# Loading queries and keys in token halves, transposing with a PSUM column step, and a shorter path for the gate's running sums

## The chip, the cores and the metric

The kernel runs on one core of a Trainium2 chip, as one program. The core has a matrix engine (TensorE, PE in the profile; its weight loads are the row PEld), three engines for elementwise work (VectorE or DVE, ScalarE or ACT, GpSimd or POOL), and SyncE (SP), which here issues almost all data transfers. Each engine takes its instructions in the order in which they were written to its queue, and waits on semaphores for the others. PSUM is the memory that PE writes its results to; ACT and DVE read it and write SBUF, from which PE reads again.

The metric is the device time of one execution in microseconds (us), median of three runs.

## The reference

Three layers follow each other. B, H, S, D = 4, 8, 576, 64.

```python
# 1. causal attention with a bias from running sums of a gate s
scores = matmul(q, k.T) / sqrt(D)
cum = cumsum(maximum(s, 0), axis=-1)
bias = -(cum[:, :, :, None] - cum[:, :, None, :])
scores = where(causal, -1e9, scores + minimum(bias, 0))
x = softmax(scores) @ v                      # -> (B, S, H*D)
# 2. gated MLP with a product over tokens
h = gelu(x @ w_in);  u, v = halves of h
v_s = einsum('ts,bsd->btd', w_sg, layernorm(v) * g_ln) + b_sg
x = x + (u * v_s) @ w_out
# 3. one of 8 experts per token; a token may reuse the choice of the token before it
e = argmax(x @ w_gate) or the previous e, by sigmoid(x @ w_local)
out = p[e] * (relu(x @ w1[e]) @ w2[e])
```

Products are computed as sums of products of a high part (type fp32r) and a remainder, so most fp32 tensors are split into `hi` and `lo`: one engine (ACT) writes `hi`, another (DVE) subtracts it from the source and writes `lo`.

## The kernel before

The 32 heads (4 batches x 8) are worked off in 16 pairs; a pair's two heads lie on partitions 0 to 63 and 64 to 127. Attention fills the first part of the program. The gated MLP of a batch (`M_steps`) and its routing (`O_steps`) are woven into the attention of the next batch, and the experts come last, from about 440 us on. The Python generators set the order in which work is emitted; the framework's scheduler then places the instructions on each engine's queue, and `behind(x, name)` tells it to place x after another instruction of the same engine.

**Loading and transposing a pair.** `prep_load(p)` loads a pair's queries and keys into the tiles `nq` and `nk`, one transfer each. Partition `p` of such a tile holds the six tokens 6p to 6p+5, so 96 partitions hold all 576 tokens. `prep_T(p, c)` (c = 0, 1) takes three of the six slots. For each of `nq` and `nk`, PE transposes the three slots into 96 columns each of a PSUM tile (L344), ACT writes the high part into the tile `qk` (L353 for queries, L356 for keys), and DVE writes the remainder (L354, L357). Since slot r of partition p is token 6p+r, the 96 columns of a slot go to every sixth token of the destination:

```python
            def v6(x):
                return x.rearrange("p (t r) -> p r t", r=6)[:, 3 * c:3 * c + 3, :]
```

So each move reads 288 columns of PSUM in a row and writes 288 elements with a step of six (24 bytes). There are 16 pairs x 2 halves x 2 tiles = 64 moves on ACT, as many on DVE, and 192 transposes on PE.

**Scores, softmax and product.** Scores of the first four pairs (batch 0) are made by `emit_R` (L466), those of the others by `emit_S` and `emit_tail` (L841, a helper's line, which is used by all later layers too). DVE takes each row's extreme (L411), ACT the exponential (L417), POOL and DVE the reciprocal of the sum (L418, L419), POOL the scaling (L420). PE transposes the result (L502); in batch 0 DVE or ACT copies it to the tile `et` (L508, L506); then PE multiplies with the values (L541).

**The gate's running sums.** Batch 0 needs its sums early: `emit_first` loads eight rows of the gate (tile `u`, L200), and makes the sums and their split (L223 to L233) with a scan along the row (L224). All other heads get theirs from `emit_cum`, at the pair p = 2: it loads all 32 heads' rows into 32 partitions, clamps (L239), scans (L241), and then for each of five query blocks subtracts the sum at the block's start, 32 partitions at a time (L246). The two results of 128 and 32 rows are split (L247 on ACT, L248 on DVE) and stored to `cum_d` in DRAM, from where the assembly of the later heads (`prep_asm`, `prep_cum`) reads.

**Other constants.** `emit_consts2` makes small constants for the routing (L309 to L330): POOL writes integers into a scratch tile, DVE converts them. They are needed only from the first `O_steps` on. W_steps also splits the 64-bit weights `w_in` (`vg`, L723 to L730) and prepares `bbc` (L1400) while batch 0's attention runs.

Of the kernel before, what the change touches and what calls it, by code (L numbers as in the profile page):

```python
# [33 lines left out]
def kernel(  # L34
# [217 lines left out]
    cum_rows = cum_d.rearrange("z (i g) s -> g (z i) s", g=NH)  # L252
    GD = H
    SW = ()

    def cblk(g):

        return 64 * (g % 2) + 16 * (g // 2)
# [1259 lines left out]
```

## Time and profile before

| | |
|---|---|
| median of 3 runs | 843.71 us (842.79 to 845.37) |
| profiled execution, its own time | 844.22 us |
| its span, first to last instruction | 842.4 us |
| mean granted TensorE clock | 0.978 of full speed |
| PE busy | 792.2 us (94%) |
| DVE, ACT, POOL busy | 532.1 (63%), 449.9 (53%), 349.1 us (41%) |

The profile is of one execution: its time less its span, 1.8 us, lies outside the first and last instruction. Busy time of an engine is the union of its instructions, and a share of the span is an average over stages that differ; a PE that is busy is not always at its peak.

### The profile page before, as it was taken

To read this page: it belongs to the slowest core of one execution; us is meant where nothing else is said; L and a number is where in the kernel's file an instruction comes from. 1 tells how busy PE (TensorE), PEld (TensorE's weight loads), DVE (VectorE), ACT (ScalarE), POOL (GpSimd) and SP (SyncE) were. 2 spreads that over 40 slices of the span, in tenths; PEclk is the share of its full clock that TensorE was granted. 3 is DMA by queue.
4 is the path that set the end of the run, shared out by engine and by line. 5 is a ranking of instruction groups with operands and counts; after the bars stand their busy time and mean duration, and the time that the engine had idled before them with its cause. 6 is when DMAs were issued, how large, how long until landed. Compare 5 with 4: busy or idle time off the path is not lost. (4 is left out here: it accounts for less than half of the span.)

```text
span 842.4 us, 14677 instructions
## 1 busy us (share of the span) xinstructions
PE 792.2 (94%) x4828; PEld 678.2 (80%) x4828; DVE 532.1 (63%) x1489; ACT 449.9 (53%) x1040; POOL 349.1 (41%) x627
## 2 busy tenths in 40 slices
PE   8797998989999999999998999989999999999995
PEld 4564687779879889878788788778989989899894
DVE  7777577876768788867786476774555444353420
ACT  5676577766637786527784245134454344443510
POOL 5785556576434387614586001052022222313101
PEclk9699999999999999999999999999999999999998
DMA  8565699794488587587450763144564544535300
GB/s 186 137 184 142 153 229 306 192 237 99 93 192 231 153 214 174 130 238 201 92 179 18 255 220 123 51 139 142 178 211 122 176 127 146 186 126 184 125 5 35
DMA packets 117735, 133.33 MB, mean 158 GB/s; under 512 B 69184, under 2 KB 82624, under 8 KB 117656
## 3 DMA queue, kind: packets, MB, share of 16 engines
q1 hardware_dynamic: 113816, 122.87, 53.6%
q0 software_dynamic: 3840, 9.48, 3.0%
q8 instruction: 40, 0.66, 0.3%
q14 instruction: 39, 0.32, 0.1%
HBM read 91.07 MB, written 23.13 MB: 136 GB/s over the span
## 5 line engine op out<-in xcount | busy, mean ns | idle before, releaser
L1211 DVE TENSOR_TENSOR wp<-wraw,wp 128x1024 fp32r<-128x1024 f32 x63 | 76.6, 1223 | 96.6 <-ACT wp L1210 96.0
L841 PE MATMUL ps<-wp,hT 128*128 128x512 f32 x528 | 123.0, 392 | 0.0
L1267 POOL DMA_INDIRECT out_dram<-y,ids x24 | 34.9, 1454 | 204.6 <-ACT y L1266 157.0
L841 PE MATMUL ps<-xT,wp 128*128 128x384 f32 x672 | 119.1, 336 | 0.0
L841 PEld LDWEIGHTS ps<-xT,wp 128*128 128x128 f32 x672 | 117.3, 188 | 0.7
L841 PEld LDWEIGHTS ps<-wp,hT 128*128 128x128 f32 x528 | 98.6, 188 | 21.1
L1210 ACT CAST wp<-wraw 128x1024 fp32r<-128x1024 f32 x64 | 66.5, 1050 | 65.3 <-DMA wraw<-in_moe_w_dram 58.6
L417 ACT ACTIVATE E<-E,negm 128x128 f32<-128x128 f32 (+4 forms) x136 | 79.1, 582 | 35.5 <-DVE negm L411 30.5
L420 POOL TENSOR_SCALAR E<-E,lsum 128x128 f32<-128x128 f32 (+4 forms) x136 | 79.6, 588 | 38.1 <-DVE lsum L419 28.4
L541 PE MATMUL ps<-et,vv 128*128 128x320 f32 (+9 forms) x476 | 82.7, 314 | 9.9 <-DVE et L508 5.7
L418 POOL TENSOR_SCALAR lsum<-lsum 128x1 f32<-128x1 f32 x144 | 34.5, 240 | 124.7 <-ACT E L417 111.2
L541 PEld LDWEIGHTS ps<-et,vv 128*128 128x128 f32 (+1 forms) x476 | 65.1, 171 | 25.1 <-ACT wsg L247 5.4
L502 PE MATMUL ps<-ident,E 128*128 128x128 f32 (+1 forms) x452 | 69.2, 266 | 8.9 <-POOL E L420 5.5
L411 DVE CUSTOM_DVE_ANT_0 E<-ps,zmask 128x128 f32<-128x128 f32 (+4 forms) x136 | 63.5, 474 | 17.8 <-PE ps L841 15.4
L841 PE MATMUL ps<-wsg,vg 128*128 128x288 f32 x448 | 68.3, 304 | 2.0 <-DVE g L850 1.0
L510 ACT CAST et<-ps 128x384 fp32r<-128x384 f32 (+3 forms) x120 | 50.6, 431 | 33.4 <-PE ps L502 31.4
L841 PEld LDWEIGHTS ps<-wsg,vg 128*128 128x128 f32 x448 | 62.3, 192 | 3.3 <-DVE g L850 1.2
L502 PEld LDWEIGHTS ps<-ident,E 128*128 128x128 f32 (+1 forms) x452 | 48.0, 142 | 20.6 <-POOL E L420 6.9
L511 DVE TENSOR_TENSOR et<-ps,et 128x384 fp32r<-128x384 f32 (+3 forms) x120 | 56.8, 483 | 7.2 <-ACT et L510 6.8
L841 PE MATMUL ps<-xh,w 128*128 128x288 f32 x256 | 57.6, 303 | 0.6 <-DVE negm L411 0.5
L1255 DVE SCALAR_TENSOR_TENSOR hT<-ps,hT 128x384 fp32r<-128x384 f32 x56 | 30.3, 553 | 40.4 <-ACT hT L1254 40.4
L841 PE MATMUL ps<-w,vg 128*128 128x512 f32 (+1 forms) x216 | 54.5, 396 | 0.0
(305 smaller groups left out, 1624.7 us busy)
## 6 DMA issues: line engine op xcount, KB each, us to landing
wraw<-in_moe_w_dram SPq DMA_DIRECT2D x64, 512.0 KB
qk<-qk SPq DMA_DIRECT2D x24, 432.0 KB
w<-wv_d SPq DMA_DIRECT2D x16, 512.0 KB
w<-wo_d SPq DMA_DIRECT2D x16, 512.0 KB
qk<-qk SPq DMA_DIRECT2D x24, 288.0 KB
w<-wu_d SPq DMA_DIRECT2D x12, 512.0 KB
nq<-in_q_dram SPq DMA_DIRECT2D x16, 288.0 KB
nk<-in_k_dram SPq DMA_DIRECT2D x16, 288.0 KB
```

The source lines that it names most:

```text
L411: hred[g] = DVE.tensor_tensor_reduce(out=e[:, a:z], in0=pt[:, 0:z - a], in1=zmask[:, m0:m0 + z - a], scale=-1.0, scalar=BIG if hi == 0 els ...
L417: ACT.activation(out=x, in_=x, func=ACTF.Exp, scale=-1.0, bias=nm, accum_out=l)
L418: POOL.tensor_scalar(out=l, in0=l, scalar1=1e-9, scalar2=0.0, op0=ALU.add, op1=ALU.add)
L420: POOL.tensor_scalar(out=x, in0=x, scalar1=l, scalar2=1.0, op0=ALU.mult, op1=ALU.mult)
L502: PE.transpose(pt[:, j * M:(j + 1) * M], e[h, 128 * j:128 * (j + 1)], ident[h, h])
L510: ACT.copy(out=dst[0], in_=src)
L511: DVE.tensor_tensor(out=dst[1], in0=src, in1=f32v(dst[0]), op=ALU.subtract)
L541: PE.matmul(x, lhsT=l, rhs=rhs if g >= F4 else f32v(rhs), start=(j == 0 and n_ == 0), stop=(j == js[-1] and n_ == len(ms) - 1),)
L841: ms = [PE.matmul(pt, lhsT=l, rhs=r, start=(first_ and x == 0), stop=(last_ and x == n - 1)) for x, (l, r) in enumerate(pairs)]
L1210: c = ACT.copy(out=w[:, 0, :], in_=r)
L1211: a = (POOL if (e, j) == (0, KD) else DVE).tensor_tensor(out=w[:, 1, :], in0=r, in1=f32v(w[:, 0, :]), op=ALU.subtract)
L1267: POOL.indirect_dma_start(out=of[:, :], out_offset=bass.IndirectOffsetOnAxis(ap=idx, axis=0), in_=y, in_offset=None, bounds_check=NT - 1, ...
```

## The change

- `prep_load` makes two transfers of each, of 288 tokens: partition p of the first half holds tokens 3p to 3p+2, and of the second half tokens 288+3p to 288+3p+2.
- `prep_T` lets the transpose of slot r write the columns r, r+3, r+6, ... of the PSUM tile (a step of 12 bytes). The PSUM columns then stand in token order, and each move reads 288 elements in a row and writes 288 in a row.
- `emit_cum` leaves out the first eight heads, which never read `cum_d`. It loads the other 24 heads' rows five times, onto 120 partitions, so one clamp, one scan, one subtraction (with a per-partition reference taken by three small operations) and one split take the place of the five subtractions and two splits. `cum_d` has 120 rows in place of 160, and is stored by one transfer.
- the DVE part of `emit_consts2` is placed behind the first pair's first row extremes (`hred[1]`).

```diff
     def emit_cum():
-        R = 128 // NH
-        s_sb = T(mp, [128, S], F32, "u2", bufs=5)[0:NH]
-        dma(s_sb, s.rearrange("b h s -> (b h) s"))
-        behind(DVE.tensor_scalar_max(out=s_sb, in0=s_sb, scalar1=0.0), hred[max(hred)].ins.name)
-        cum = s_sb
-        DVE.tensor_tensor_scan(out=cum, data0=one[0:NH], data1=s_sb, initial=0.0, op0=ALU.mult, op1=ALU.add)
-        for P, i0, z0 in ((128, 0, 6), (NH, R, 8)):
-            tmp = T(mp, [128, S], F32, "u2", bufs=5)
-            ch = wsg[0:P, z0:z0 + 2, :]
-            for a in range(P // NH):
-                DVE.tensor_scalar(out=tmp[NH * a:NH * a + NH], in0=cum, scalar1=cum[:, 128 * (i0 + a):128 * (i0 + a) + 1], scalar2=None, op0=ALU.subtract)
-            ACT.copy(out=ch[:, 0, :], in_=tmp[0:P])
-            DVE.tensor_tensor(out=ch[:, 1, :], in0=tmp[0:P], in1=f32v(ch[:, 0, :]), op=ALU.subtract)
-            dma(cum_d[:, NH * i0:NH * i0 + P, :].rearrange("z p s -> p z s"), ch)
+        n = NH - H
+        P = NQ * n
+        rows, cum = [T(mp, [128, S], F32, "u2", bufs=5)[0:P] for _ in range(2)]
+        src = s.rearrange("b h s -> (b h) s")[H:NH]
+        for i in range(NQ):
+            dma(rows[n * i:n * i + n], src)
+        behind(DVE.tensor_scalar_max(out=rows, in0=rows, scalar1=0.0), hred[max(hred)].ins.name)
+        DVE.tensor_tensor_scan(out=cum, data0=one[0:P], data1=rows, initial=0.0, op0=ALU.mult, op1=ALU.add)
+        m = T(mp, [128, NQ], F32, "m5")[0:P]
+        ref = T(mp, [128, 1], F32, "mr")[0:P]
+        DVE.tensor_reduce(out=m, in_=ident[0:P, 0:P].rearrange("p (i c) -> p i c", c=n), axis=AX.X, op=ALU.add)
+        DVE.tensor_tensor(out=m, in0=cum.rearrange("p (i c) -> p i c", c=64)[:, 0::2, 0], in1=m, op=ALU.mult)
+        DVE.tensor_reduce(out=ref, in_=m, axis=AX.X, op=ALU.add)
+        DVE.tensor_scalar(out=rows, in0=cum, scalar1=ref, scalar2=None, op0=ALU.subtract)
+        ch = wsg[0:P, 6:8, :]
+        ACT.copy(out=ch[:, 0, :], in_=rows)
+        DVE.tensor_tensor(out=ch[:, 1, :], in0=rows, in1=f32v(ch[:, 0, :]), op=ALU.subtract)
+        dma(cum_d.rearrange("z p s -> p z s"), ch)
...
             t = T(ap_, [96, 6, 2, D], F32, nm)
-            dma(t, src[b, h0:h0 + 2].rearrange("h (p r) d -> p r h d", p=96))
+            for a in range(2):
+                dma(t[:, 3 * a:3 * a + 3], src[b, h0:h0 + 2, HS * a:HS * a + HS].rearrange("h (p r) d -> p r h d", p=96))
...
     def emit_consts2():
+        def late_(x):
+            behind(x, hred[1].ins.name)
...
-        DVE.tensor_copy(out=w8d, in_=it[:, 0:8])
+        late_(DVE.tensor_copy(out=w8d, in_=it[:, 0:8]))
...
             for r in range(3):
-                PE.transpose(pt[:, 96 * r:96 * r + 96], n[:, 3 * c + r].rearrange("p h d -> p (h d)"), ident[0:96, 0:96])
-
-            def v6(x):
-                return x.rearrange("p (t r) -> p r t", r=6)[:, 3 * c:3 * c + 3, :]
-
-            src = pt[:, 0:HS].rearrange("p (r t) -> p r t", r=3)
-            hi = v6(t[:, a, :])
-            lo = v6(t[:, 2 + a, :])
+                PE.transpose(
+                    pt[:, 0:HS].rearrange("p (t r) -> p r t", r=3)[:, r], n[:, 3 * c + r].rearrange("p h d -> p (h d)"), ident[0:96, 0:96]
+                )
+            src = pt[:, 0:HS]
+            hi, lo = [t[:, z, HS * c:HS * c + HS] for z in (a, 2 + a)]
```

The line numbers of the changed kernel are one lower in this region (L353 and L356 are its DVE moves, L410 the row extremes, L507 the copies to `et`, L729 the remainder of the weights' split) and by a few more in `emit_cum` and `emit_consts2`.

**Place 1: DVE at `emit_cum`.** Before, from the clamp of the rows (L239) to the copies that feed the next product (L508):

```order
L239 TENSOR_SCALAR u_142_890<-u_142_890 32x576
L508 COPY et_425<-ps 128x3x128
L241 SCALAR_TENSOR_TENSOR u_142_890<-u_38_148,u_142_890 32x576
L730 TENSOR_TENSOR vg_831<-vg_831 128x512
L411 ISA E_148_946,negm_948<-ps,zmask_73 128x512
L246 TENSOR_SCALAR u_143_894<-u_142_890 32x576 x3
L246 TENSOR_SCALAR u_143_894<-u_142_890 32x576
L246 TENSOR_SCALAR u_144_902<-u_142_890 32x576
L411 ISA ga_947,negm_949<-ps,zmask_73 128x512
L508 COPY et_425<-ps 128x5x64
L508 COPY et_425<-ps 128x128
```

The same place in the changed kernel:

```order
L242 TENSOR_SCALAR u_142_898<-u_142_898 120x576
L507 COPY et_431<-ps 128x3x128
L243 SCALAR_TENSOR_TENSOR u_143_899<-u_38_150,u_142_898 120x576
L729 TENSOR_TENSOR vg_839<-vg_839 128x512
L410 ISA E_149_957,negm_959<-ps,zmask_73 128x512
L247 TENSOR_TENSOR m_144_907<-u_143_899,m_144_907 120x5
L410 ISA ga_958,negm_960<-ps,zmask_73 128x512
L507 COPY et_431<-ps 128x5x64
L507 COPY et_431<-ps 128x128
L410 ISA E_28_100,negm_995<-ps,zmask_73 128x288
L248 TENSOR_REDUCE mr_908<-m_144_907 120x1
L249 TENSOR_SCALAR u_142_898<-u_143_899,mr_908 120x576
```

The five subtractions L246 are gone from ahead of the two copies to `et`; one small product stands there, and the single subtraction (L249) comes behind the copies.

**Place 2: SP's queue at the start.** Before (`u` is the gate's rows, `vg` the weights w_in, `vv`, `vt` and `vr` values):

```order
L78 DMA nq_134<-in_q_dram 96x12x64
L78 DMA nk_136<-in_k_dram 96x12x64
L200 DMA u_39_159<-in_s_dram 16x576 x8
L78 DMA vt_105<-in_v_dram 64x4x64
L78 DMA nq_227<-in_q_dram 96x12x64
L78 DMA nk_229<-in_k_dram 96x12x64
L78 DMA vg_363<-in_moe_w_in_dram 128x1024
L78 DMA u_142_890<-in_s_dram 32x576
L78 DMA bbc_75<-in_moe_b_sg_dram 128x576
L78 DMA nq_384<-in_q_dram 96x12x64
L78 DMA nk_386<-in_k_dram 96x12x64
L78 DMA vg_542<-in_moe_w_in_dram 128x1024
```

In the changed kernel (the same stretch; rows that repeat others are left out in both):

```order
L78 DMA nq_134<-in_q_dram 96x6x64 x2
L78 DMA nk_137<-in_k_dram 96x6x64 x2
L200 DMA u_39_161<-in_s_dram 16x576 x8
L78 DMA nq_229<-in_q_dram 96x6x64 x2
L78 DMA nk_232<-in_k_dram 96x6x64 x2
L78 DMA vt_105<-in_v_dram 64x4x64
L78 DMA vg_367<-in_moe_w_in_dram 128x1024
L78 DMA nq_388<-in_q_dram 96x6x64 x2
L78 DMA nk_391<-in_k_dram 96x6x64 x2
L78 DMA u_142_898<-in_s_dram 24x576 x5
L78 DMA bbc_75<-in_moe_b_sg_dram 128x576
L78 DMA vg_548<-in_moe_w_in_dram 128x1024
```

Two more issues stand ahead of the gate's eight rows, twelve more ahead of `bbc`, and ten more ahead of the fourth piece of w_in. Over the whole program SP issues 35 transfers more.

**Place 3: DVE from the first moves to the gate's split.** Before, the sums' clamp (L223) and scan (L224) stand among moves and constants:

```order
L354 SCALAR_TENSOR_TENSOR qk_25_97<-ps,qk_25_97 128x3x96
L309 CAST w8d_78<-ga_268 128x8
L357 TENSOR_TENSOR qk_25_97<-ps,qk_25_97 128x3x96
L312 CAST io_8_79<-ga_268 128x128
L223 TENSOR_SCALAR u_39_159<-u_39_159 128x576
L354 SCALAR_TENSOR_TENSOR qk_25_97<-ps,qk_25_97 128x3x96
L313 CAST ioc_80<-ga_268 128x144
L357 TENSOR_TENSOR qk_25_97<-ps,qk_25_97 128x3x96
L321 TENSOR_SCALAR ltri_86<-io_8_79,pidx_81 128x128
L224 SCALAR_TENSOR_TENSOR u_40_160<-u_38_148,u_39_159 128x576
```

In the changed kernel the moves come first, and the constants after the first row extremes:

```order
L353 SCALAR_TENSOR_TENSOR qk_25_97<-ps,qk_25_97 128x288
L356 TENSOR_TENSOR qk_25_97<-ps,qk_25_97 128x288
L223 TENSOR_SCALAR u_39_161<-u_39_161 128x576
L224 SCALAR_TENSOR_TENSOR u_40_162<-u_38_150,u_39_161 128x576
L233 SCALAR_TENSOR_TENSOR wsg_149<-wsg_149,m_45_175,u_41_163 128x576
L410 ISA E_55_245,negm_247<-ps,zmask_73 128x128
L311 CAST w8d_78<-ga_272 128x8
L314 CAST io_8_79<-ga_272 128x128
L315 CAST ioc_80<-ga_272 128x144
L323 TENSOR_SCALAR ltri_86<-io_8_79,pidx_81 128x128
```

All four moves of the first pair now stand ahead of the clamp, and none of the eleven constants.

## Rows read from the trace of the kernel before

**Rows 1.** Windows: us, then PE, PEld, DVE, ACT, POOL busy, clock, DMA, GB/s.

```profile
0.00:100.00 100.00, 84.40 (x480) 55.20 (x481) 70.98 (x230) 62.23 (x157) 66.82 (x143) 0.90 0.66 159
100.00:440.00 340.00, 322.78 (x2222) 282.20 (x2221) 262.61 (x845) 228.54 (x608) 191.33 (x403) 0.99 0.72 185
440.00:842.40 402.40, 384.98 (x2131) 340.74 (x2129) 198.53 (x415) 159.15 (x275) 91.00 (x84) 0.99 0.42 135
```

**Rows 2.** ACT by shapes: xcount | busy us, mean ns | idle before.

```profile
L356 ACT CAST qk<-ps 128x288 fp32r<-128x288 f32 x32 | 24.3, 758 | 0.9 <-PE ps L344 0.9
L353 ACT ACTIVATE qk<-ps 128x288 fp32r<-128x288 f32 x32 | 22.5, 704 | 7.2 <-PE ps L344 5.9 <-POOL lsum L418 1.0
...
L510 ACT CAST et<-ps 128x320 fp32r<-128x320 f32 x24 | 10.2, 425 | 10.9 <-PE ps L502 9.5 <-PE ps L541 1.1
...
L510 ACT CAST et<-ps 128x256 fp32r<-128x256 f32 x24 | 8.9, 371 | 0.2
```

**Rows 3.** DVE by shapes, the same columns.

```profile
L354 DVE SCALAR_TENSOR_TENSOR qk<-ps,qk 128x288 fp32r<-128x288 f32 x32 | 22.6, 707 | 6.6 <-ACT qk L353 6.3
L357 DVE TENSOR_TENSOR qk<-ps,qk 128x288 fp32r<-128x288 f32 x32 | 22.2, 694 | 0.7 <-ACT qk L356 0.7
...
L511 DVE TENSOR_TENSOR et<-ps,et 128x320 fp32r<-128x320 f32 x24 | 11.6, 483 | 3.7 <-ACT et L510 3.4
...
L511 DVE TENSOR_TENSOR et<-ps,et 128x256 fp32r<-128x256 f32 x24 | 10.0, 418 | 0.3 <-ACT et L510 0.3
```

**Rows 4.** PE's waits, 0 to 100 us: us in total, times, longest.

```profile
PE ps L541 <- DVE et L508: 5.7, 2, 5.2
...
PE ps L466 <- DVE qk L354: 1.4, 2, 1.1
```

**Rows 5.** DVE in order of time at `emit_cum`: start us, us, instruction.

```profile
67.72 1.60 DVE L246 TENSOR_SCALAR u<-u 32x576 f32<-32x576 f32 x3
...
69.54 1.27 DVE L246 TENSOR_SCALAR u<-u 32x576 f32<-32x576 f32 x2
...
71.34 0.67 DVE L508 COPY et<-ps 128x320 f32<-128x320 f32 x2
```

**Rows 6.** PE in order of time, 66 to 84 us; in brackets its idle time before.

```profile
71.96 3.61 PE L541 MATMUL ps<-et,vv 128*64 128x320 f32 x10 [5.19 <-DVE et L508]
...
77.73 0.41 PE L344 MATMUL ps<-ident,nq 96*128 96x96 f32 x3
...
83.53 2.27 PE L541 MATMUL ps<-et,vv 128*64 128x320 f32 x10
```

**Rows 7.** Window of that product; columns as in rows 1.

```profile
71.90:75.50 3.60, 3.54 (x10) 1.80 (x10) 2.44 (x10) 1.23 (x4) 2.82 (x4) 0.61 0.41 157
```

**Rows 8.** SP's issues in order of time, first 26 us.

```profile
2.31 4.43 SPq L200 DMA_DIRECT2D u<-in_s_dram  x8
...
7.63 0.61 SPq L78 DMA_DIRECT2D nq<-in_q_dram  x1
...
16.48 2.62 SPq L78 DMA_DIRECT2D bbc<-in_moe_b_sg_dram  x1
```

**Rows 9.** DVE in order of time, 6 to 27 us.

```profile
6.96 0.16 DVE L309 CAST w8d<-ga 128x8 f32<-128x8 int32 x1
...
8.74 0.45 DVE L223 TENSOR_SCALAR u<-u 128x576 f32<-128x576 f32 x1
...
12.16 0.17 DVE L319 CAST wtok<-ga 128x20 f32<-128x20 int32 x1
...
13.70 0.82 DVE L233 SCALAR_TENSOR_TENSOR wsg<-wsg,m,u 128x576 fp32r<-128x576 f32 x1 [0.18 <-ACT wsg L231]
...
25.45 1.44 DVE L1400 TENSOR_SCALAR bbc<-bbc 128x576 f32<-128x576 f32 x1
```

**Rows 10.** Window of the weights' split beside batch 0; columns as in rows 1.

```profile
17.00:37.40 20.40, 14.87 (x79) 10.77 (x78) 19.55 (x57) 15.01 (x40) 18.37 (x31) 0.67 0.61 142
```

**Rows 11.** Transposes of queries: duration ns min/median/max, first and last start.

```profile
L344 PE MATMUL ps<-ident,nq x96: 243/246/423, 4.9 to 411.0; 96*128 96x96 f32 x96
```

More of the change, by code (lines that the diff above doesn't have):

```diff
@@ L188 @@
     vt = T(ap_, [128, 4, D], F32, "vt")
-    cum_d = dram.tile([2, NQ * NH, S], F32, name="cum_d")
+    cum_d = dram.tile([2, NQ * (NH - H), S], F32, name="cum_d")
     def slot(z, dt=F32R):
@@ L197, in emit_first @@
         rows, cum, t1 = [T(mp, [128, S], F32, "u2", bufs=5) for _ in range(3)]
-        for g in range(GD):
-            z = cblk(g)
-            (POOL if g in SW else SP).dma_start(out=rows[z:z + 16], in_=s[0, g:g + 1, :].to_broadcast([16, S]))
+        for g in range(H):
+            z = 64 * (g % 2) + 16 * (g // 2)
+            SP.dma_start(out=rows[z:z + 16], in_=s[0, g:g + 1, :].to_broadcast([16, S]))
         e = [T(mp, [128, NQ], F32, f"e{z}") for z in range(3)]
@@ L251 @@
-    KX = 64 + 2 * NQ
[L252 to L258, printed above, removed]
+        n = NH - H
[5 more added lines that the diff above has]
+        behind(DVE.tensor_scalar_max(out=rows, in0=rows, scalar1=0.0), hred[max(hred)].ins.name)
@@ L260 @@
+        ch = wsg[0:P, 6:8, :]
+        ACT.copy(out=ch[:, 0, :], in_=rows)
+        DVE.tensor_tensor(out=ch[:, 1, :], in0=rows, in1=f32v(ch[:, 0, :]), op=ALU.subtract)
+        dma(cum_d.rearrange("z p s -> p z s"), ch)
+    KX = 64 + 2 * NQ
+    cum_rows = cum_d.rearrange("z (i g) s -> g (z i) s", g=NH - H)
     last = {(PR - 2 + z) % 2: 2 * PR - 3 + 2 * z for z in range(2)}
@@ L308, in emit_consts2 @@
         POOL.iota(it[:, 320:320 + B * NQ], pattern=[[-S, B], [-128, NQ]], base=FREE, channel_multiplier=-1)
-        DVE.tensor_copy(out=w8d, in_=it[:, 0:8])
-        DVE.tensor_copy(out=s8, in_=it[:, 8:8 + NQ])
-        DVE.tensor_copy(out=pidx, in_=it[:, 16:17])
-        DVE.tensor_copy(out=io128, in_=it[:, 32:160])
-        DVE.tensor_copy(out=ioc, in_=it[:, 160:160 + NC])
+        late_(DVE.tensor_copy(out=w8d, in_=it[:, 0:8]))
+        late_(DVE.tensor_copy(out=s8, in_=it[:, 8:8 + NQ]))
+        late_(DVE.tensor_copy(out=pidx, in_=it[:, 16:17]))
+        late_(DVE.tensor_copy(out=io128, in_=it[:, 32:160]))
+        late_(DVE.tensor_copy(out=ioc, in_=it[:, 160:160 + NC]))
         tk = it[:, 320:320 + B * NQ]
         hl = it[:, 384:384 + B * NQ]
-        DVE.tensor_scalar(out=hl, in0=tk, scalar1=6, scalar2=None, op0=ALU.logical_shift_right)
-        DVE.tensor_copy(out=wtok[:, 0], in_=hl)
-        DVE.tensor_scalar(out=tk, in0=tk, scalar1=63, scalar2=None, op0=ALU.bitwise_and)
-        DVE.tensor_copy(out=wtok[:, 1], in_=tk)
-        DVE.tensor_scalar(out=first, in0=s8, scalar1=9.0, scalar2=None, op0=ALU.is_equal)
-        DVE.tensor_scalar(out=ltri, in0=io128, scalar1=pidx, scalar2=None, op0=ALU.is_gt)
+        late_(DVE.tensor_scalar(out=hl, in0=tk, scalar1=6, scalar2=None, op0=ALU.logical_shift_right))
+        late_(DVE.tensor_copy(out=wtok[:, 0], in_=hl))
+        late_(DVE.tensor_scalar(out=tk, in0=tk, scalar1=63, scalar2=None, op0=ALU.bitwise_and))
+        late_(DVE.tensor_copy(out=wtok[:, 1], in_=tk))
+        late_(DVE.tensor_scalar(out=first, in0=s8, scalar1=9.0, scalar2=None, op0=ALU.is_equal))
+        late_(DVE.tensor_scalar(out=ltri, in0=io128, scalar1=pidx, scalar2=None, op0=ALU.is_gt))
         POOL.memset(onesb, 1.0)
@@ L327, in emit_consts2 @@
         n = E + 1
-        DVE.tensor_tensor(out=ii, in0=ident[0:2 * n, 0:n], in1=ident[0:2 * n, n:2 * n], op=ALU.add)
+        late_(DVE.tensor_tensor(out=ii, in0=ident[0:2 * n, 0:n], in1=ident[0:2 * n, n:2 * n], op=ALU.add))
         dma_after(1, gcol, g_ln.rearrange("(k p) -> p k", p=128))
-        DVE.tensor_scalar(out=gcol, in0=gcol, scalar1=0.5, scalar2=None, op0=ALU.mult)
+        late_(DVE.tensor_scalar(out=gcol, in0=gcol, scalar1=0.5, scalar2=None, op0=ALU.mult))
     Tst = {}
@@ L366, in prep_asm @@
         rs = slice(64 * r, 64 * r + 64)
-        dma(dst[64:KX, 3, :], cum_rows[g])
+        dma(dst[64:KX, 3, :], cum_rows[g - H])
         if buf[g] not in selected:
@@ L377, in prep_cum @@
         for r in range(2):
-            dma(czp[64 * r:64 * r + 2, :], cum_rows[2 * p + r, NQ - 1::NQ, :])
+            dma(czp[64 * r:64 * r + 2, :], cum_rows[2 * p + r - H, NQ - 1::NQ, :])
     VG = 4
```

## The prediction

> **What bounds the kernel now.** I read the windows by stage first: PE is busy for 84.4 + 322.8 + 385.0 = 792.2 us, 94% of the span [rows 1]. A shorter instruction on DVE or ACT therefore gains only where PE is seen to wait for it, and an instruction that gets longer on PE costs nearly its full length. The same windows say where waits are: of the first 100 us PE is idle for 15.6 (100 less 84.4), of the 340 us up to 440 for 17.2, and behind that for 17.4 of 402 in the experts, which the change doesn't touch [rows 1]. DVE is busy for 71% of the first stage and 77% of the second, so these two are where DVE's queue can hold PE up. The chain of waits ends in the experts' last store and says nothing of attention, so I went to PE's waits in the first 100 us: the longest is for copies to `et` by DVE, and a smaller sum is for the transposed queries [rows 4].
>
> **The moves.** 64 moves on each of ACT and DVE write with a step before and in a row after. The trace has no move of 288 columns in a row into fp32r from PSUM; the copies to `et` bracket it, of 256 and 320 columns. On ACT these take 371 and 425 ns, so I take 398 for 288, against 704 and 758: 306 and 360 less, over 32 of each 21.3 us of ACT's time [rows 2]. On DVE 418 and 483 ns give 450 against 707 and 694: 257 and 244 less, 16.0 us [rows 3]. From below, a move might be bound by reading PSUM and not get faster at all; the copies read PSUM too, so I keep this only as a rival.
>
> Most of this lies beside a busy PE. In the first 100 us PE waited for the moves directly 1.4 us in two waits, of 1.1 and 0.3 [rows 4]. Each stands behind one move on ACT and one on DVE in series, about 0.6 together, so the first loses 0.6 and the second all of its 0.3: **0.9 us**. From 100 to 440 us no single wait is the moves' own. Eleven pairs take 11 us off DVE's 262.6 and 14.6 off ACT's 228.5, 4 and 6% of queues that PE waits for. As a share of the 17.2 us of idle that is about 0.9; if one DVE move of each half pair lay on the path it would be 11 x 2 x 0.25 = 5.5; from below it is nothing. I take **1.5**, near the share, since PE's idle there is many short waits.
>
> **The running sums.** PE stood for 5.19 us ahead of the product at 71.96 until DVE had made its copies [rows 6]. DVE was not waiting: from 67.72 it ran five subtractions, one reciprocal and a row extreme, and only then the copies at 71.34 [rows 5]. In the changed order (place 1) no subtraction is left ahead of the copies. The block from 67.72 to 69.54 + 1.27 = 70.81 goes, 3.1 us. The reciprocal in it stays (the gap between the two rows, 0.2), and a product of 120x5 comes in, about 0.17 by the nearest small operation, L319 [rows 9]. The copies come **2.6 us** earlier, and PE with them. Scan and clamp cost the same on more partitions by the clamp of `emit_first`, 0.45 us on 128 [rows 9]. What is late next is the later split and the store to `cum_d`: the subtraction, ACT's copy and the remainder still end sooner than two splits did. I bound this term by 1.5, if another engine holds the copies once DVE is free, and 3.5.
>
> **The clock.** The product behind that wait took 3.61 us; the same ten matmuls took 2.27 us at 83.53 [rows 6]. The first ran with a granted clock of 0.61 on average, so for most of it at the lower of PE's two levels, 1.2 GHz, after the idle stretch [rows 7]. If a wait of 2.6 us is short enough, up to 1.34 us come back; if not, nothing. I take **0.7**.
>
> **The start.** Two more issues stand ahead of the gate's rows (place 2). A half's issue isn't in the trace; a whole one took 0.61 and a row of the gate 4.43/8 = 0.55 [rows 8], so the rows may land 1.2 us later and the clamp L223 moves from 8.74 to 9.9. From the clamp to the end of L233 it was 5.8 us (13.70 + 0.82 less 8.74) [rows 9]. In this stretch stood two moves of 0.7 and eight of the eleven constants, which lie between 0.16 at 6.96 and 0.17 at 12.16 [rows 9], about 0.17 each; one shorter move is left (place 3). That makes 5.8 - 1.4 - 1.4 + 0.45 = 3.5, and L233 ends at 13.4, 1.1 earlier. But the constants come back behind the first extremes: 11 x 0.17 = 1.9 on a DVE that is then busy for 19.55 of 20.40 us up to 37.4, with PE's clock at 0.67 [rows 10]. Four moves in that stretch give 1.0 back. So far -1.1 + 1.9 - 1.0 = -0.2.
>
> Then SP. Twelve more issues, 6.6 us at 0.55, stand ahead of `bbc`, whose own took 2.62 from 16.48 [rows 8]; it would end at 25.7, and its reader stood at 25.45 [rows 9]. The reader moves behind the next piece of the weights, some 2 to 3 us later. Behind it DVE holds row extremes and copies that PE needs, and the fourth piece of w_in comes ten issues later too. I put 0.6 on this, 0 to 2.5. The start in all: **0.4 us slower**, between 1.0 faster and 2.5 slower.
>
> **Nothing for** the 26 further halves and the smaller store: SP is idle between issues later on, and loads are a pair ahead of their transposes. If that cover went, a transpose would wait for a load by the 0.61 us of one more issue, thirteen times.
>
> **The sum:** 0.9 + 1.5 + 2.6 + 0.7 - 0.4 = 5.3 us. The profiled execution took 844.22 (span 842.4 and 1.8 around it), 0.5 above the median of 843.71; 843.7 - 5.3 is **838.4**. Its bounds don't meet all at once: 834 to 842 as its own range.
>
> **Transposes and PSUM's step, the rival on the other side.** 192 transposes now write every third column. Three in a row take 0.41 us and one alone 0.246 [rows 6, 11], so one adds 0.082 us. No row of this kernel has PE write PSUM with a step, so the bounds are no cost and, if every column took its place alone and twice as long, 0.082 x 192 = 15.7 us. PE is busy for nine tenths of these stretches [rows 1], so 14 of it would count: 838.4 + 14 = 852. It decides from 5.3/(192 x 0.9) = 31 ns each, three in a row in 0.50 us. For it speaks that nothing hides it. Against it: a column comes every 0.85 ns in a transpose (0.082 us over 96), and every 0.71 ns in the product of 10 x 320 columns in 2.27 us [rows 6], so the transposes do not press the port even now. I take no cost in the sum, and a chance of 0.15 for this.
>
> The Trainium skill, page "PSUM — Partial Sum Buffer", section "Specifications (TRN2)", says that PSUM has lines of 8 bytes and that any access pattern that isn't contiguous slows matmuls significantly. By that rule the rival happens and the time is around 852; no run before shows it either way.
>
> **Rival: the start takes it back.** `bbc`, the weights and the returned constants hold DVE up by their 2.5 us, and the second stage gains nothing, since its waits are other operations': 843.7 - 0.9 - 2.6 + 2.5 is 842.7, or about 843 with a slower restart. For it speaks rows 10: DVE has no slack to 37.4. Against it, the reader of `bbc` moves back too. Chance 0.14.
>
> **Rival: the moves get no faster.** If reading PSUM and not the step sets their 700 ns, only the sums' terms are left: 843.7 - 2.6 - 0.7 + 0.4 + 1.0 (the four moves) is 841.8. The copies to `et`, which read as much in 60% of the time, speak against it. Chance 0.04.
>
> **Rival: more.** If DVE's and ACT's shorter queues halve PE's idle in the second stage (8.6 us in place of 1.5), the time is 831. The shares of 4 and 6% speak against. Chance 0.09.
>
> **How the numbers follow.** The main case has 0.58. A difference of 0.3%, 2.5 us, is about what a measurement of this kernel tells from none, so faster is below 841.2 and slower above 846.2. Faster: 0.54 of the main case, 0.09 and 0.01 of the third rival, 0.64. Same: 0.04, 0.13 and 0.03, 0.20. Slower: 0.15 and 0.01, 0.16. The range of 832 to 847 leaves out the transposes' case and the lower half of "more", 0.19.
>
> **What would show it.** The moves at about 400 ns on ACT and 450 on DVE; PE's wait ahead of the ten matmuls of L541 at 2.6 us or less in place of 5.19, and these ten in 2.3 to 3.6; three transposes still in 0.41; the first row extreme about a microsecond earlier than before, and DVE at 37 us no further behind. Wrong would be: a triple of transposes over 0.5, a DVE that waits for `bbc` or a piece of w_in between 25 and 33 us, or a wait for the copies that another engine now ends.

## The result, and the profile after

The changed kernel took **837.01 us** (median of five runs, 834.58 to 838.24) against 845.37 for the kernel before in runs beside it: a ratio of **0.9891**, with a 95% interval of 0.9866 to 0.9916, so 7 to 11 us less. Forecast were 838.4 and 5.3 less. The profiled execution took 834.58 us, with a span of 832.7 against 842.4.

The engines' line of the page, and three stages as in [rows 1] (the last stretch ends with the span). Columns of a window: us; busy time of PE, PEld, DVE, ACT and POOL; granted clock; DMA share; GB/s.

```profile
PE 788.3 (95%) x4828; PEld 677.6 (81%) x4828; DVE 512.7 (62%) x1487; ACT 436.6 (52%) x1039; POOL 341.6 (41%) x627
...
0.00:100.00 100.00, 84.88 (x492) 56.09 (x493) 66.29 (x232) 58.41 (x158) 67.06 (x145) 0.90 0.64 159
100.00:440.00 340.00, 327.19 (x2277) 289.21 (x2276) 255.23 (x863) 224.62 (x624) 198.28 (x412) 0.99 0.70 187
440.00:832.70 392.70, 376.21 (x2064) 332.34 (x2062) 191.21 (x394) 153.55 (x259) 76.27 (x71) 0.99 0.43 137
```

From 100 to 440 us PE is now idle for 12.8 us (340 less 327.19) where it was 17.2. The window counts 2277 matmuls where it held 2222 [rows 1]; since later work moves into it, I measured stretches between the same matmuls in the experiments.

Groups of the moves and transposes by shape: busy time, mean ns of one, idle time just before.

```profile
L353 DVE SCALAR_TENSOR_TENSOR qk<-ps,qk 128x288 fp32r<-128x288 f32 x32 | 14.4, 449 | 3.0 <-ACT qk L352 2.9
L356 DVE TENSOR_TENSOR qk<-ps,qk 128x288 fp32r<-128x288 f32 x32 | 14.3, 447 | 3.7 <-ACT qk L355 3.7
L346 PE MATMUL ps<-ident,nq 96*128 96x96 f32 x96 | 14.0, 255 | 0.0
...
L352 ACT ACTIVATE qk<-ps 128x288 fp32r<-128x288 f32 x32 | 13.0, 407 | 9.3 <-PE ps L346 7.4 <-issue 1.6
L355 ACT CAST qk<-ps 128x288 fp32r<-128x288 f32 x32 | 12.7, 398 | 2.2 <-PE ps L346 2.2
```

The moves take what the copies of [rows 2, 3] promised: 398 to 449 ns where they took 694 to 758. The transposes, which now write every third column of PSUM, cost nothing more: 255 ns on average, and the row below shows three in 0.41 us, as in [rows 6]. PE in order of time, with the restart that was 71.96 in [rows 6], and PE's longest waits in the first 100 us (total, times, longest):

```profile
70.74 3.12 PE L540 MATMUL ps<-et,vv 128*64 128x320 f32 x10 [2.31 <-DVE et L507]
...
76.43 0.41 PE L346 MATMUL ps<-ident,nq 96*128 96x96 f32 x3
```

```profile
PE ps L501 <- POOL E L419: 5.8, 2, 3.3
PE ps L540 <- DVE et L507: 4.8, 3, 2.3
PE ps L346 <- DMA nk<-in_k_dram: 1.1, 1, 1.1
```

The wait ahead of the ten matmuls fell from 5.19 to 2.31. The sum of PE's waits for `et` fell less, from 5.7 to 4.8 [rows 4], because two others took some back. One more row, DVE's at `bbc`, is a wait that [rows 9] did not have:

```profile
31.89 0.46 DVE L1399 TENSOR_SCALAR bbc<-bbc 128x576 f32<-128x576 f32 x1 [2.10 <-DMA bbc<-in_moe_b_sg_dram]
```

**Where the 9.7 us of the spans came from.** I looked up the same matmul in both traces. Place A is a product with `wsg` (65.95 before), B a product with `xl` (110.01), C the last transposes of `xf` before the experts (418.50).

| | A | A to B | B to C | C to the end of the span |
|---|---|---|---|---|
| before | 65.95 | 44.06 | 308.49 | 423.9 |
| after | 67.61 | 40.27 | 301.38 | 423.4 |
| gained | -1.66 | 3.79 | **7.11** | 0.5 |

The start lost 1.7, the stretch with the running sums gave 3.8, and the second stage 7.1. Three questions came of that: is the second stage's gain the moves' time, or the halved loads, or the order that the scheduler makes of the changed program? Are the sums worth their 3.8? And is the start's loss real?

### The profile page after: what moved, and what is told of

Read it like the earlier page. It is cut to its first block, busy times and chain, and to the rows that moved or that the text cites. A ratio compares the mean times of both kernels' runs of the same rounds, so it can differ in the third digit from the quotient of the medians.

```text
span 832.7 us, 14728 instructions
## 1 busy us (share of the span) xinstructions
PE 788.3 (95%) x4828; PEld 677.6 (81%) x4828; DVE 512.7 (62%) x1487; ACT 436.6 (52%) x1039; POOL 341.6 (41%) x627
## 5 line engine op out<-in xcount | busy, mean ns | idle before, releaser
L1266 POOL DMA_INDIRECT out_dram<-y,ids x24 | 30.6, 1274 | 211.2 <-ACT y L1265 170.4
L410 DVE CUSTOM_DVE_ANT_0 E<-ps,zmask 128x128 f32<-128x128 f32 (+4 forms) x136 | 63.7, 471 | 17.5 <-PE ps L840 13.3
```

Source lines behind the costliest of these rows:

```text
L410: hred[g] = DVE.tensor_tensor_reduce(out=e[:, a:z], in0=pt[:, 0:z - a], in1=zmask[:, m0:m0 + z - a], scale=-1.0, scalar=BIG if hi == 0 els ...
L1266: POOL.indirect_dma_start(out=of[:, :], out_offset=bass.IndirectOffsetOnAxis(ap=idx, axis=0), in_=y, in_offset=None, bounds_check=NT - 1, ...
```

## The experiments

Each ratio is to the kernel before, run beside it on the same chip; the rows come from several chips. This table answers for each run: mean ns of the moves on ACT and on DVE, places and stretches as above, the granted clock from B to C (these from one profiled execution), and the ratio with its interval. The clock bears on B to C: in the traces compared below a stretch at the lower level costs about 1.5 us, and a hundredth of the column is about two of them.

| run | ACT, DVE ns | A | A to B | B to C | clock | ratio |
|---|---|---|---|---|---|---|
| before | 731, 700 | 65.95 | 44.06 | 308.49 | 0.99 | 1 |
| after | 402, 448 | 67.61 | 40.27 | 301.38 | 0.99 | 0.9891 (0.9866 to 0.9916) |
| after again | 402, 448 | 65.19 | 40.95 | 301.49 | 0.99 | 0.9869 (0.9831 to 0.9908) |
| old moves | 731, 702 | 64.56 | 42.15 | 311.73 | 0.97 | 0.9968 (0.9945 to 0.9992) |
| old sums | 403, 448 | 64.01 | 42.88 | 301.64 | 0.99 | 0.9910 (0.9876 to 0.9944) |
| early constants | 402, 448 | 64.51 | 41.53 | 301.24 | 1.00 | 0.9899 (0.9853 to 0.9945) |
| late bbc | 401, 448 | 66.78 | 42.69 | 309.95 | 0.98 | 0.9930 (0.9904 to 0.9957) |
| step of 3 | 562, 546 | 66.83 | 42.70 | 301.16 | 1.00 | 0.9880 (0.9843 to 0.9917) |
| step on reads | 403, 448 | 68.23 | 41.39 | 299.55 | 0.99 | 0.9897 (0.9859 to 0.9935) |
| one sums load | 403, 448 | 68.04 | 41.82 | 302.12 | 0.98 | 0.9875 (0.9839 to 0.9912) |
| step of 6 | 727, 704 | 66.46 | 43.87 | 307.10 | 0.98 | 0.9959 (0.9937 to 0.9981) |
| before, runs of 3 | 462, 455 | 64.97 | 43.93 | 305.14 | 0.99 | 0.9931 (0.9897 to 0.9965) |
| whole loads | 402, 448 | 64.29 | 41.14 | 302.82 | 0.99 | 0.9890 (0.9856 to 0.9924) |
| one sums load, early constants | 403, 448 | 64.89 | 40.97 | 313.40 | 0.96 | 0.9898 (0.9849 to 0.9946) |

### Undoing one part each

**Old moves.** `prep_load` and `prep_T` as before, the rest changed:

```diff
-            for a in range(2):
-                dma(t[:, 3 * a:3 * a + 3], src[b, h0:h0 + 2, HS * a:HS * a + HS].rearrange(...))
+            dma(t, src[b, h0:h0 + 2].rearrange("h (p r) d -> p r h d", p=96))
...
+            hi = v6(t[:, a, :])
+            lo = v6(t[:, 2 + a, :])
```

> The changed kernel with the loads, transposes and moves of the kernel before; sums and constants stay changed. Theory (the shorter moves bring the gain between 100 and 440 us, about 7.7 us, and the sums about 3 with the clock): the sums' gain stays and the returned constants cost up to 2, so a ratio to before of 0.996 to 0.999, 841 to 844 us, moves at 700 to 760 ns again, and PE idle for 16 us or more from 100 to 440 us. Rival (the order of instructions, or the smaller sums, brings the gain of the second stage): ratio of about 0.990, PE idle for about 13 us there. Second rival (the start's loss comes from the constants and not from the loads): PE's position at 30 us still 1.5 to 2 us behind that of before; by the theory of the loads on SP it is within 0.7 us of it.

Measured: 844.62 us, 0.9968. The whole gain of the second stage is gone (B to C 311.73, longer than before, at a lower clock too), so loads and moves together bring it, and the sums and constants do not. They are worth 0.1 to 0.55% by themselves. PE at 33 us stood 1.0 behind that of before, between the two theories of the start.

**Old sums.** `emit_cum`, `cum_d` and its readers as before:

```diff
-    cum_d = dram.tile([2, NQ * (NH - H), S], F32, name="cum_d")
+    cum_d = dram.tile([2, NQ * NH, S], F32, name="cum_d")
...
-        for i in range(NQ):
-            dma(rows[n * i:n * i + n], src)
+        dma(s_sb, s.rearrange("b h s -> (b h) s"))
```

> The changed kernel with the running sums of the kernel before (160 rows in two splits, and the larger store). Theory: only the sums' term is lost, 2.9 us of waiting and about 0.5 of clock; ratio to before 0.992 to 0.995 (838 to 840 us), PE waits about 5 us for the copies to et near 72 us, and the gain from 100 to 440 us stays at 7 us or so. Rival (the sums also free the second stage, through the store of 10 rows a head less or the scheduler's order): ratio above 0.997.

Measured: 838.7 us, within the forecast of 838 to 840; the ratio of 0.9910 is a little below the forecast 0.992 to 0.995, and its interval holds the changed kernel's ratio too. So the sums' worth is not told from nothing by times. In its trace PE waited 4.23 us for the copies (4.2 to 5.2 in the three traces with the old sums, 1.8 to 2.3 in all those with the new), and B to C kept its gain.

**Early constants.** Without the rule that holds them back:

```diff
         def late_(x):
-            behind(x, hred[1].ins.name)
+            return x
```

> The changed kernel without the rule that holds the constants behind the second row extreme. Theory (the loss at the start is bbc's late landing and SP's issues): the constants go back between the moves, the first row extreme comes 0.5 to 1.5 us later, DVE still waits about 2 us for bbc, and the time stays within 0.3% of the changed kernel, ratio to before 0.988 to 0.993. Rival (the constants behind the extremes cost the start its 1.6 us): 1.5 us or more faster than the changed kernel, ratio about 0.987, and PE at 40 us no longer behind that of before.

Measured: 837.27 us, 0.9899, the same as the changed kernel. DVE waited 2.48 us for `bbc`, as the theory of the start had it, but PE, which stood 0.8 behind before at 33 us, was 1.4 ahead of it at A (64.51). The first row extreme, forecast 0.5 to 1.5 us later, came at the same time (15.33, after 15.34). In the times an effect of 1.5 us is less than this interval could show.

**Late bbc.** DVE's multiplication of `bbc` placed behind a later row extreme:

```diff
         dma_after('last', bbc, b_sg.unsqueeze(0).to_broadcast([128, S]))
-        DVE.tensor_scalar(out=bbc, in0=bbc, scalar1=0.5, scalar2=None, op0=ALU.mult)
...
         yield from emit_w_sg()
+        behind(DVE.tensor_scalar(out=bbc, in0=bbc, scalar1=0.5, scalar2=None, op0=ALU.mult), hred[max(hred)].ins.name)
```

> The changed kernel with DVE's multiplication of bbc placed much later, behind a row extreme that is issued after the shared gate's weights, instead of at 29.8 us. Theory (DVE stands 2.1 us for bbc with extremes and copies behind it, and PE waits for those): PE's waits at 34.75 and 49.22 us get shorter by 1.5 to 2 us together, PE at 45 us stands at most 0.5 us behind that of before, and the time falls by about 1.5 us; ratio to before 0.986 to 0.988. Rival (DVE would only stand for the next piece of the weights, or PE has the time to spare later): same as the changed kernel, 0.989 to 0.991.

Measured: 840.93 us, 0.9930; above both forecasts, not faster and perhaps slower than the changed kernel. Why is not known; the scheduler placed other instructions anew as well. The profiled execution (846.74 us) met a late transfer of weights: DVE stood for it, and PE's next product waited 4.61 us behind. Its B to C is spoilt by that and says nothing of the moves. DVE in order of time:

```profile
153.72 0.43 DVE L723 TENSOR_SCALAR vg<-vg 128x512 int32<-128x512 int32 x1 [3.93 <-DMA vg<-in_moe_w_out_dram]
```

### One duration at a time, in one order

The edits so far let the scheduler place things anew. The next ones, but for the last, were chosen so that every instruction stands where it stood, on PE, DVE, ACT, POOL and SP.

**After again**, as the anchor.

> The changed kernel itself again, as the anchor on the chip of the three others: a ratio to before of 0.987 to 0.992 by both theories. Its trace shows how far one execution's waits stand from another's: at 25 to 65 us PE's place is expected within 3 us of the first trace, and the gain from 100 to 440 us between 5 and 8.

Measured: 834.91 us, 0.9869. B to C is 301.49, within 0.1 of the first trace. A is 65.19 where it was 67.61, and DVE did not wait for `bbc` at all: two executions of one kernel differ at the start by more than the loss that I had read from the first.

**Step of 3.** The moves alone go through a view of every third column:

```diff
+            def v3(x):
+                return x.rearrange("p (t r) -> p r t", r=3)
+            sv, hv, lv = v3(src), v3(hi), v3(lo)
...
-                ACT.mul(out=hi, in_=src, mul=0.125)
+                ACT.mul(out=hv, in_=sv, mul=0.125)
```

and so the other three moves.

> The changed kernel in which the moves alone go through a view that reads and writes every third column (12 bytes in SBUF and in PSUM) in place of a row; loads by halves, transposes, sums, constants and the order of every instruction on every engine are those of the changed kernel. Theory (what counts is how long the moves last): moves at 650 to 760 ns, PE idle for 15 to 17 us from 100 to 440 us in place of 12.8, ratio 0.995 to 0.998. Rival (the halved loads and the order that the scheduler makes of the program bring the gain): moves slow but ratio still 0.988 to 0.992. A third way: a step of 12 bytes costs less than one of 24, moves near 500 ns, and the ratio in between.

Measured: 837.85 us, 0.9880, and B to C 301.16. The moves cost 550 ns, near the third way, but the ratio was that of the rival, halves and order, unless 550 ns was short enough. Two things weaken that reading: this trace had no stretch at the lower clock between B and C, where after again had two, and the ratio's interval reaches 0.9917, where a part of the gain would be lost. A step of 6 had to decide.

**Step of 6.** The same with `r=6`, which writes with the 24 bytes of the kernel before:

> As the run with moves through a view, but of every sixth column (24 bytes, the step of the kernel before), in the changed kernel's order of instructions and with its loads by halves. If the moves' time brings the second stage's gain and 550 ns was short enough: moves at 650 to 760 ns, PE idle for 15 to 17 us from 100 to 440 us, ratio 0.994 to 0.998. If the order or the halves bring it: the same moves, but PE idle for 12 to 14 us there and a ratio of 0.987 to 0.991.

Measured: 843.27 us, 0.9959; moves at 698 to 752 ns. Its interval does not touch those of after again, step of 3 and whole loads (the last on the same chip, 6.5 us faster). Same order, same halves, same loads as after again: **the moves' time brings the gain**, some 6 to 8 us of it by these ratios. PE's idle time in the window was no good sign (13.4 us, which spoke for the rival): a matmul in a stretch at the lower clock counts as busy, and the window holds 39 matmuls fewer. The step of 6, and then after again:

```profile
100.00:440.00 340.00, 326.65 (x2236) 286.56 (x2234) 261.01 (x848) 229.75 (x609) 193.70 (x406) 0.98 0.70 186
```

```profile
100.00:440.00 340.00, 327.16 (x2275) 289.41 (x2274) 254.75 (x862) 224.20 (x622) 199.50 (x413) 0.99 0.70 187
```

The stretch B to C, 307.10 against 301.49, shows the difference. Groups by shape in this run:

```profile
L360 ACT CAST qk<-ps 128x288 fp32r<-128x288 f32 x32 | 24.1, 752 | 0.9 <-PE ps L346 0.9
L358 DVE SCALAR_TENSOR_TENSOR qk<-ps,qk 128x288 fp32r<-128x288 f32 x32 | 22.7, 710 | 5.9 <-ACT qk L357 5.3
```

Since the order is the same, the two traces can be read side by side. The step of 6, PE and then DVE in order of time:

```profile
230.01 0.41 PE L506 MATMUL ps<-ident,E 128*128 128x128 f32 x2 [0.36 <-DVE am L1023]
230.77 0.39 PE L545 MATMUL ps<-et,vv 128*128 128x320 f32 x1 [0.35 <-ACT qk L357]
...
233.17 0.38 PE L1032 MATMUL rt<-ident,code 128*5 128x128 f32 x2 [0.31 <-DVE code L1028]
```

```profile
229.78 0.19 DVE L1023 TENSOR_REDUCE am<-eq 128x5 f32<-128x40 f32 x1
...
229.96 0.66 DVE L361 TENSOR_TENSOR qk<-ps,qk 128x288 fp32r<-128x288 f32 x1
...
231.53 0.73 DVE L358 SCALAR_TENSOR_TENSOR qk<-ps,qk 128x288 fp32r<-128x288 f32 x1
232.15 0.69 DVE L361 TENSOR_TENSOR qk<-ps,qk 128x288 fp32r<-128x288 f32 x1
...
232.96 0.15 DVE L1028 TENSOR_TENSOR code<-code,fz 128x5 f32<-128x5 f32 x1
```

The same places in the changed kernel (after again):

```profile
223.65 0.41 PE L501 MATMUL ps<-ident,E 128*128 128x128 f32 x2
224.21 0.39 PE L540 MATMUL ps<-et,vv 128*128 128x320 f32 x1
...
226.22 0.39 PE L1027 MATMUL rt<-ident,code 128*5 128x128 f32 x2
```

```profile
223.42 0.19 DVE L1018 TENSOR_REDUCE am<-eq 128x5 f32<-128x40 f32 x1
...
223.60 0.46 DVE L356 TENSOR_TENSOR qk<-ps,qk 128x288 fp32r<-128x288 f32 x1
...
224.96 0.45 DVE L353 SCALAR_TENSOR_TENSOR qk<-ps,qk 128x288 fp32r<-128x288 f32 x1
225.33 0.45 DVE L356 TENSOR_TENSOR qk<-ps,qk 128x288 fp32r<-128x288 f32 x1
...
225.89 0.15 DVE L1023 TENSOR_TENSOR code<-code,fz 128x5 f32<-128x5 f32 x1
```

PE waits for `code`, a product of five columns. From `am` to `code` DVE takes 3.18 us in the one and 2.47 in the other; between them stand three moves of 2.08 together against 1.36. The difference is all theirs, and the wait carries another name. From 195 us to C the changed kernel gains 4.2 us, with as many stretches at the lower clock in the one as in the other. I found thirteen places there at which PE goes on 0.16 to 0.40 us sooner, 3.8 us in all, and one at which it goes on 0.45 later. Most are about a move's saving long. Seven are named `mv`, `am`, `code`, `xf`, `negm` or `et`, two a move itself, and the others have no named wait. Between B and 195 us, where the other 1.5 us lie, gains and losses mix, and the clock gives more than that. In the step of 6, products of 512 columns behind 171 us start 0.42 us apart that start 0.22 apart in the other. Two such stretches (granted 0.50 from 140 to 142 us, 0.52 from 172 to 174), at whose places after again had 1.00, cost 1.5 us each, and longer waits of after again took about half back. Whether longer moves bring more such stretches is open: over all executions the mean granted clock was 0.977 in the step of 6, and 0.977, 0.980 and 0.979 in after, after again and whole loads.

**Before, runs of 3.** The crossed case: the order and loads of before, and moves that walk their columns as runs of three:

```diff
-                return x.rearrange("p (t r) -> p r t", r=6)[:, 3 * c:3 * c + 3, :]
+                return x.rearrange("p (t r) -> p t r", r=6)[:, :, 3 * c:3 * c + 3]
...
-            src = pt[:, 0:HS].rearrange("p (r t) -> p r t", r=3)
+            src = pt[:, 0:HS].rearrange("p (r t) -> p t r", r=3)
```

> The kernel before, with its order of instructions on every engine and its loads, in which the moves alone walk their columns in another order: they write runs of three columns and then skip three, and read PSUM with a step. Moves expected at 400 to 600 ns. If the moves' time brings the second stage's gain: PE idle for 12 to 14 us from 100 to 440 us in place of 17.2, ratio 0.990 to 0.994. If the order or the halves bring it: PE idle for 16 us or more, ratio 0.997 to 1.001.

Measured: 841.69 us, 0.9931, moves at 453 to 470 ns. So the old order gains with the moves as well, though PE's idle time of 15.9 us from 100 to 440 us lies between the two forecasts. Its trace gained 4.2 us behind 233 us (`code` to C, 180.98 against 185.15) and lost 0.8 ahead of it, where DVE stood 2.73 us for a transfer of weights.

**Whole loads.** One transfer of queries and one of keys in place of two halves:

```diff
-            for a in range(2):
-                dma(t[:, 3 * a:3 * a + 3], ...)
+            dma(t, src[b, h0:h0 + 2].rearrange("h (p r) d -> p r h d", p=96))
```

> The changed kernel with queries and keys loaded whole, by one transfer each, as before; transposes and moves as changed, so the columns stand for other tokens (the output is not the reference's, the work is the same). If the moves' time counts: moves at 400 and 450 ns and a ratio of 0.986 to 0.991, PE idle for 12 to 14 us from 100 to 440 us. If the loads by halves bring the second stage's gain: ratio 0.994 to 0.998 with moves just as short. For the start, 26 issues fewer: DVE's wait for bbc 0 to 1.2 us in place of 2.1.

Measured: 836.81 us, 0.9890, B to C 302.82: the gain stays without the halves, and in another order, since the scheduler moved some instructions here. The halves are only the price of getting tokens into order, and no cost of theirs is seen.

### PSUM's step, and the start

**Step on reads.** PE writes in a row, and the moves read PSUM by columns 96 apart:

```diff
-                PE.transpose(pt[:, 0:HS].rearrange("p (t r) -> p r t", r=3)[:, r], ...)
+                PE.transpose(pt[:, 96 * r:96 * r + 96], ...)
...
-            src = pt[:, 0:HS]
-            hi, lo = [t[:, z, HS * c:HS * c + HS] for z in (a, 2 + a)]
+            src = pt[:, 0:HS].rearrange("p (r t) -> p t r", r=3)
+            hi, lo = [t[:, z, HS * c:HS * c + HS].rearrange("p (t r) -> p t r", r=3) for z in (a, 2 + a)]
```

The new view of `hi` and `lo` still goes through them in a row.

> The changed kernel with the step moved from PE's writes to the moves' reads of PSUM: transposes write 96 columns in a row, moves read PSUM by columns 96 apart and write SBUF in a row, same order of instructions. Theory (neither side of PSUM minds a step, only writes to SBUF do): transposes 0.41 us for three, moves at 400 and 450 ns, ratio as the changed kernel, 0.987 to 0.992. Rival (reads of PSUM with a step are slow, and the step on PE's writes is what makes the moves fast): moves at 600 ns or more, ratio 0.994 to 0.998.

Measured: 838.38 us, 0.9897, the same; moves at 398 to 450 ns. Neither PE's writes nor the moves' reads of PSUM show a cost of a step here: the starts of neighbouring transposes lie 82 to 83 ns apart (median) in before, after and this run. What made the moves slow was the step in SBUF. On ACT, which reads PSUM alone, that is the step on the write; DVE's moves also read `hi` from SBUF with the same step, and no run tells its read from its write. Groups by shape:

```profile
L351 DVE SCALAR_TENSOR_TENSOR qk<-ps,qk 128x288 fp32r<-128x288 f32 x32 | 14.4, 450 | 5.7 <-ACT qk L350 5.4
...
L350 ACT ACTIVATE qk<-ps 128x288 fp32r<-128x288 f32 x32 | 13.1, 408 | 11.9 <-PE ps L346 10.5 <-issue 1.0
```

The Trainium skill, page "PSUM — Partial Sum Buffer", section "Specifications (TRN2)", says that any pattern that isn't contiguous slows matmuls significantly; for these transposes the measurement differs (three in 0.41 us with the step and without). The Trainium skill, page "SBUF — State Buffer", section "Specifications (TRN2)", gives SBUF lines of 16 bytes, a penalty for each crossing and full bandwidth from two hits per line; the moves agree (a row 0.40 us on ACT, a step of 12 bytes 0.56, of 24 bytes 0.73).

**One sums load.** One transfer of 120 rows in place of five of 24:

```diff
-        for i in range(NQ):
-            dma(rows[n * i:n * i + n], src)
+        dma(rows, src.unsqueeze(0).to_broadcast([NQ, n, S]))
```

> The changed kernel with the rows of the running sums loaded by one transfer of 120 rows in place of five of 24; the order of everything else is the same. Theory (the four further issues, some 2.2 us of SP ahead of bbc and the fourth piece of the weights, are the start's loss): bbc's issue at about 24.5 us in place of 26.75, DVE waits for bbc for 0 to 0.9 us in place of 2.1, PE at 33 to 45 us 1 to 2.5 us earlier than in the changed kernel, and most of it kept: ratio 0.985 to 0.989. Rival (bbc's own landing of about 5 us or the constants hold the start up): DVE's wait falls by less than 0.7 us and the time is the same.

Measured: 837.29 us, 0.9875, no different from after again on the same chip. `bbc` was issued at 24.42, as forecast, and DVE did not wait for it; but it did not wait in after again either, issued at 25.05. Nor does this execution test the theory: PE ran at about half its rate for longer at its start than in after again (last section), so DVE came to `bbc` only at 32.64 (29.40 there), and the place of PE at 33 us can't be read.

**One sums load and early constants**, the two edits together.

> The changed kernel with one load for the running sums' rows and without the rule that holds the constants back: the version that both theories of the start would favour. If SP's issues and the constants are what the start loses, PE at 45 to 66 us stands 2 us ahead of that of before at the least (read only if PE is at full speed as early as in before), ratio 0.982 to 0.988. If the sums' loads have cover anyway, 0.986 to 0.992.

Measured: 841.45 us (830.98 to 847.32), 0.9898 with a wide interval: inconclusive. Its profiled execution lost its time where PE fell to the lower clock (0.58 granted from 180 to 190 us), so neither it nor its C can be set against the others. A lies ahead of that: 64.89, 1.1 ahead of before, where 2 at least were forecast. No version here is shown to beat the changed kernel.

## Why the prediction was right, and which terms were not

The sign, the mechanism and the time (838.4 against 837.01) held; two terms of the sum were mis-sized, and a third could not be settled. That the time came so near is in part luck. The gain was 8.4 us against a forecast of 5.3, but the kernel before was 1.7 us slower in the runs beside it than in those that the forecast started from. And the first trace gave 2.1 us up to B where the terms of that part make 3.8, which hid some of what the moves' term lacked (after again gave 3.9).

- **Moves, 100 to 440 us: predicted 1.5, measured 5.6 to 7.** B to C gained 7.1 and 7.0 in two traces, of which 5.6, the clock's part included, go with the moves' time alone (the step of 6 against after again, one trace each). By the ratios all the moves are worth 6 to 8 us, where the two terms made 2.4. This is the step that failed: "I take 1.5, near the share". The share of DVE's and ACT's busy time says nothing of a queue in which PE's short waits come one after another. The upper bound beside it, 5.5 for one DVE move of each half pair on the path, came near: thirteen places, about a move's saving each, and beside them the clock. The remark that "no single wait is the moves' own" was wrong even by the names. The trace of before has three such waits there, 0.8 us in all:

```profile
PE ps L841 <- DVE qk L357: 0.5, 2, 0.2
...
PE ps L541 <- ACT qk L353: 0.3, 1, 0.3
```

Others carry another name; ahead of `code` stood three moves. The rival "more", with a chance of 0.09, took 8.6 us in place of 1.5 and was nearer in size, though PE's idle time fell by 4.4 us and not by half. Whether moves at 550 ns give all of the gain or a part is open (0.9880, 0.9843 to 0.9917). With moves as long as before, the changed order kept 1.4 of the 7 (step of 6); that is no gain of the moves and no more than traces differ by.
- **Moves in the first 100 us, 0.9.** PE's waits under the names of the moves fell from 1.4 and 0.3 us to 0.2 and 0.5 there, and one of 1.1 for the keys' load came in. So it may have given the 0.9 or nothing; it wasn't tried apart.
- **The sums, 2.6.** The rows that it names give 2.7. The wait fell by 2.88 us, 5.19 to 2.31, and was 2.29 to 2.30 in nine other traces of the new sums (1.76 in one). The mechanism was seen as put. What it is worth in time stays open: with and without, the intervals overlap.
- **The clock, 0.7.** Not borne out. Behind the same wait of 2.3 us the ten matmuls took 2.24, 3.12, 3.53 and up to 4.29 us in different traces, and 3.61 to 4.28 behind one of 5.2. A shorter wait does not decide at which of the two levels, 1.2 or 2.4 GHz, PE goes on.
- **The start, 0.4 slower.** Six and not eight of the constants stood in the stretch that the prediction counts, and the first row extreme came 0.2 and 0.5 us earlier in the two traces, not about 1. The first trace lost 1.7 at A, with DVE's wait for `bbc` that the prediction had named. Over four executions of the changed order (after, after again, the two steps) A lies between 65.19 and 67.61, so the loss is between -0.8 and 1.7, within the range as predicted. In a fifth, step on reads, A stood at 68.23 behind a longer start at half rate. In the four, A follows the wait: 65.19 and 66.46 without one, 66.83 with 1.6 us, 67.61 with 2.1; SP issued `bbc` at 25.05, 24.86, 26.25 and 26.75. But early constants waited 2.48 and stood ahead of before at A, and the two edits that were to test it fell into executions with a longer start at half rate. So the theory that the loss is `bbc` behind SP's issues is neither shown nor refuted.
- **Nothing for the halves:** whole loads gave the same ratio.
- **The rival of PSUM's step** did not happen: 0.41 us for three transposes, where 0.50 would have decided.

## What to carry to other kernels

A transposed tile can be put into its final order by PE's write to PSUM, or by the mover's read of it, and neither showed a cost here; the step in SBUF was what cost, at 24 bytes a factor of 1.8 on ACT and 1.6 on DVE. When PE's idle time is made of many waits of a few tenths, do not price a shorter instruction by its share of busy time: go through the queue of the engine that is waited for, count how often the instruction stands between the last release and the one that PE waits for, and take its saving each time; here that came near (5.5 against 5.6 to 7), the share did not. To tell a duration from an order, change the duration alone in a kernel whose instructions stay where they are.

## What was not expected of the hardware

**PE at half its rate under a granted clock of 1.00.** In all fourteen profiled executions the first warm-up products of 512 columns start about 0.43 us apart, and later ones 0.22 apart, while the clock column says 1.00 from the start. The time of the change differs from execution to execution: in eleven it came between 3.5 and 7 us, in three (late bbc, step on reads, one sums load) at about 13 us. The run with one sums load, a window and rows of PE in order of time:

```profile
4.00:8.00 4.00, 3.64 (x15) 1.70 (x13) 1.23 (x3) 1.92 (x5) 3.75 (x19) 1.00 0.61 145
```

```profile
0.93 4.02 PE L158 MATMUL rt<-warm 128*32 128x512 bf16 x9 [0.93 <-DVE cf L1038]
...
6.51 0.69 PE L345 MATMUL ps<-ident,nq 96*128 96x96 f32 x3
7.13 1.46 PE L158 MATMUL rt<-warm 128*32 128x512 bf16 x3
```

After again, the same:

```profile
4.00:8.00 4.00, 3.45 (x23) 1.75 (x22) 1.33 (x4) 2.21 (x6) 3.75 (x19) 1.00 0.62 135
```

```profile
0.93 3.74 PE L158 MATMUL rt<-warm 128*32 128x512 bf16 x9 [0.93 <-DVE cf L1039]
...
5.92 0.41 PE L346 MATMUL ps<-ident,nq 96*128 96x96 f32 x3
6.26 0.82 PE L158 MATMUL rt<-warm 128*32 128x512 bf16 x3
```

The instructions of PE and their order are the same, three warm-up products take 1.46 or 0.82 us, and the clock column says 1.00 in both. At the start of this program that column alone can't be trusted; the durations of equal matmuls can. The later change puts PE 3.7 us later (16.01 against 12.35 for one and the same matmul), more than several of the effects that were asked for here.

**A step in SBUF, by engine.** 288 elements from PSUM to SBUF as fp32r (on DVE with `hi` read from SBUF at the same step): in a row 402 ns on ACT and 448 on DVE (means of the two moves), in runs of three with gaps of three 462 and 455, every third element 562 and 546, every sixth 727 and 704. ACT is the faster of the two in a row and the slower with a step.
